# Zeros of a kernel's second sums: one transfer at the end of attention, or twelve pieces along its steps

## The chip, the cores and the metric

The kernel runs on one core of a Trainium2 chip. The metric is the device time of one execution in microseconds (us); less is better. Engines are named as in the profile: PE (TensorE), DVE (VectorE), ACT (ScalarE), POOL (GpSimd) and SP (SyncE, which here only issues DMAs). PEld are PE's weight loads. DMAs are issued from SP, from ACT and, for gathers and scatters, from POOL.

## What is computed

Attention of two kinds is added up (a local one with a band of 7 keys, and one over q, k and v averaged by fours). Its output, 2304 rows of 512, goes through a mixture of experts that takes two of eight experts for each row, and then through a second one that takes one of eight.

```python
def reference(**kwargs):
    attn_out = _attn_ref(**attn_kwargs)               # [4, 8, 576, 64], local + pooled attention
    x = attn_out.transpose(0, 2, 1, 3).reshape(2304, 512)
    x = _moe_ref(x=x, **moe_kwargs)                   # 8 experts, top 2: sum of w * relu(x @ w1[e]) @ w2[e]
    return _moe2_ref(x=x, **moe2_kwargs)              # 8 experts, top 1, with a bias by modality
```

## The kernel before

**Data in DRAM.** `x_rows` (line 878) takes attention's output, a row for each token, and the weights of its two experts. `x2_rows` (line 879), 2944 rows of 516 floats (2304 tokens and 640 spare rows; 2064 bytes each), takes the sums of the first mixture: each expert's results are added to it by scatters that accumulate (line 1220). So it has to hold zeros before the first scatter. In the profile both tensors carry the name `x_rows`. The zeros come from an SBUF tile `zero` that POOL fills at the start (line 936).

**Attention** runs over 16 pairs of heads. Step i of the loop at line 1116 (i from 0 to 17) transposes q and k of pair i+1 (line 193), makes the scores of pair i (lines 211 to 222), the softmax of pair i (`softmax1`, `softmax_d1`, `softmax_d2`) and of i-1 (`softmax2`), and the product with v of pair i-2 (`values`, line 315). Two pairs are a group g; there are eight groups. PE, ACT, DVE and POOL work on a step in turn: PE scores, DVE maxima, ACT exponentials, POOL products (line 269), PE transposes of these (line 283), and so on. In odd steps the loads for the next groups are written: v for the averaged form (`vr`, line 142), and q and k of group g+2 (`qk`: ten DMAs, lines 129 and 132; those of line 132 hold the last 64 positions of all four heads). In even steps v for the local form follows (`vw`, line 156). `group(g+1)` in even steps is the first to use a group's q and k: four transposes of the last 64 positions (line 166), PE's `prs`. A few small inputs are loaded in steps 3 to 7 (lines 923 to 931).

From step 6 on, finished rows of tokens go out: PE transposes them (`px`, line 965), ACT copies them (`xr`, line 986, two buffers; `xrs` for the last five tiles) and issues the write to `x_rows` itself (line 990). The first half's routing (`route1`: DVE, with POOL's help) runs from step 12 on, and SP writes its weights `wb` behind it (line 1031). Behind attention POOL gathers the first expert's rows from `x_rows` (line 709), and the mixture begins: PE transposes of the gathered rows (line 718), ACT `xh` (line 720), and matrix products (lines 735 and 748) to the end of the kernel. Of its weights the first two quarters (`raw`, lines 683 and 684) are loaded by SP as step 14 writes them, and are split into two parts at line 695 (`whi`).

**What sets the order.** The order on each engine is that in which the code is written. SP's queue is one, and in order: a load that waits holds back all that stand behind it. The DMAs of SP and ACT share eight semaphores, taken in turn along the program; a DMA is issued when the one that had its semaphore before has landed, be it of SP or of ACT. SP runs ahead of the other engines by about a step.

**Where the zeros stand.** The whole of `x2_rows` is written with one DMA of SP in step 14, behind the first weights (line 1186). The spare rows of `x_rows` get theirs in step 12 (line 1178).

Of the kernel before, what the change touches and what calls it, by code (L numbers as in the profile page):

```python
# [372 lines left out]
def finish_now(gen):  # L373

    while True:
        try:
            next(gen)
        except StopIteration as e:
            return e.value
# [155 lines left out]
class Items:  # L535
# [94 lines left out]
    def next(self):  # L630

        nc, w, tag, nt = self.nc, self.consts, self.tag, self.nt
        m = w.tile([128, self.most], F32, tag=f"{tag}nm", name="nm")
        j = w.tile([128, self.most], F32, tag=f"{tag}nj", name="nj")
        r = w.tile([128, 1 + nt], F32, tag=f"{tag}nr", name="nr")
        ei = w.tile([128, 1], I32, tag=f"{tag}nei", name="nei")
        nc.vector.tensor_scalar(m, self.ij, self.count, None, op0=ALU.is_equal)
        for a, src in enumerate([self.ei] + [self.col[:, a] for a in range(nt)]):
            nc.vector.tensor_tensor(j, m, src, op=ALU.mult)
            nc.vector.tensor_reduce(r[:, a:a + 1], j, axis=AX.X, op=ALU.add)  # L640
        nc.vector.tensor_copy(ei, r[:, 0:1])
        nc.vector.tensor_scalar(self.count, self.count, 1.0, None, op0=ALU.add)
        return dict(e=ei[0:1], e128=r[:, 0:1], col=[r[:, 1 + a:2 + a] for a in range(nt)])
# [220 lines left out]
def core(ctx, tc, q, k, v, moe_w_gate, moe_w_noise, moe_noise, moe_w1, moe_w2,  # L864
         moe2_modality_id, moe2_w_gate, moe2_modality_bias, moe2_w1, moe2_w2, out):
    nc = tc.nc
# [3 lines left out]
    NT = N // 128  # L870
# [3 lines left out]
    XW, YW = DM + 2 * E, DM + 4  # L874
# [4 lines left out]
    x2_rows = dram.tile([N + 640, YW], F32, tag="x2_rows", name="x2_rows")  # L879
# [29 lines left out]
    with ExitStack() as actx:  # L909
# [25 lines left out]
        zero = consts.tile([128, XW], F32, tag="zero", name="zero")  # L935
# [25 lines left out]
        def xback(t, halves):  # L961

            for o, b, s, n in pieces(t):
                for j in range(4):
                    nc.tensor.matmul(halves[j // 2][o:o + n, j % 2], att.xT[b][:, j, s:s + n], gw[:, j], start=True, stop=True)
            if t < 13:
                return axr.tile([128, 2, 2, 128], F32, tag="xr", name="xr")

            if t == 13:
                many.append(att.sb.tile([128, 5, 2, 2, 128], F32, tag="qk", name="xrs", bufs=2))  # L970

            return many[0][:, NT - 1 - t]
# [3 lines left out]
        def flush():  # L976
            while after:
                after.pop(0)()

        def xback_att(t):  # L980
            px = att.psD.tile([128, 2, 512], F32, tag="D", name="px")
            pv = px[:, :, :2 * XB].rearrange("p a (b c) -> p a b c", b=2)
            xr = xback(t, [pv[:, 0], pv[:, 1]])

            def rest():
                nc.scalar.activation(xr, pv[:, :, :, :128], AF.Copy)
                lgs = axr.tile([128, 2, 2, 2 * E], F32, tag="lgs", name="lgs")
                nc.scalar.activation(lgs, pv[:, :, :, 128:], AF.Copy)
                nc.vector.tensor_reduce(lg[:, t], lgs.rearrange("p a b c -> p c a b"), axis=AX.XY, op=ALU.add)
                nc.scalar.dma_start(x_rows[128 * t:128 * t + 128, :DM], xr.rearrange("p a b c -> p (a b c)"))  # L990
            after.append(rest)
# [63 lines left out]
        def tick(n=1, pe=False):  # L1055

            if pe:
                wait[0] = False
            while n and back and not wait[0]:
                n -= 1  # L1060
                try:
                    what = next(back[0])
                    wait[0] = what in ("PE", "PE soon") and not pe
                    age[0] = 2 if what == "PE soon" else 0
                except StopIteration:
                    back.pop(0)

        def unblock(lag=0):

            if wait[0]:  # L1070
                if age[0] < lag:
                    age[0] += 1
                else:
                    wait[0] = False
                    tick(1)
# [20 lines left out]
        def places_early():  # L1096

            v, f = (t.rearrange("p (e t) -> p e t", e=E)[:, :NX, :NE0] for t in (tab, fs))
            yield from rt.decode(f, v, rt.padh.rearrange("p (e t) -> p e t", e=E)[:, :NX, :NE0])
            nc.vector.tensor_copy(idx0[:, 0], f)  # L1100

            d = route.tile([128, NX, NE0], F32, tag="hold2", name="hold2")
            nc.vector.tensor_scalar(d, f, float(N), -float(N), op0=ALU.is_ge, op1=ALU.mult)
            yield
            nc.vector.tensor_tensor(idx0[:, 1], d, f, op=ALU.add)
            yield
# [9 lines left out]
        for i in range(NP + 2):  # L1116
            g, ph = divmod(i, 2)
            if ph == 1:
                if g + 1 < 2 * B:
                    att.load_vr(g + 1)  # L1120
                if g + 2 < 2 * B:
                    att.load_qk(g + 2)
            if ph == 0 and i and g < 2 * B:
                att.load_vw(g)
            if 3 <= i <= 7:
                next(small, None)
            if i == NP - 1:
                att.pool_v(g, 1)
            if i + 1 < NP:
                if i == 0:  # L1130
                    att.scores(i)
                    att.softmax1(i)
                tr = att.transposes(i + 1)
                next(tr)
            if 1 <= i <= NP:
                att.softmax2(i - 1)
            if i + 1 < NP:
                finish_now(tr)
            if i >= 2:
                att.values(i - 2)  # L1140
                att.scale_d(i - 2)
            flush()
            if i == 12:
                back.append(route1(0, HT, att_bank, nc.vector, nc.gpsimd, hold))
                back.append(places_early())
            unblock(1)
            if i in before:
                xback_att(before[i])
            if 0 < i < NP:
                att.scores(i)  # L1150
            if i >= 2:
                att.combine(i - 2)
            flush()
            tick(2)
            if 1 <= i <= NP:
                pt = att.p_transposes(i - 1)
                next(pt)
            if 0 < i < NP:
                att.softmax1(i)
            if 1 <= i <= NP:  # L1160
                finish_now(pt)
            unblock(1)
            if i < NP:
                att.softmax_d1(i)
                if ph == 0 and g + 1 < 2 * B:
                    att.group(g + 1)
                att.softmax_d2(i)
                for c in ((0,), (1,))[ph] if i > 1 else ((), (0, 1))[ph]:
                    if i < NP - 1:
                        att.pool_v(g, c)  # L1170
            tick(2 if i < NP else 30)
            if i == 9:
                second_bias()
            if i in behind:
                xback_att(behind[i])
            if i == 12:

                nc.sync.dma_start(x_rows[N:].rearrange("(a p) c -> p a c", p=128),
                                  zero[:, None, :].to_broadcast([128, 5, XW]))
            if i == 14:  # L1180
                ffn.begin([dict(e=e, ns=n, w1=moe_w1, w2=moe_w2) for e, n in
                           [(e, EARLY) for e in range(NX)] + [(e, CAP - EARLY) for e in range(NX)]
                           + [(e, CAP) for e in range(NX, LAST)] + [(LAST, 640)]]
                          + [dict(ns=n, w1=moe2_w1, w2=moe2_w2) for n in [512, 256, 256, 384] + [256] * (STATIC - 1)])

                nc.sync.dma_start(x2_rows.rearrange("(a p) c -> p a c", p=128),
                                  zero[:, None, :YW].to_broadcast([128, NT + 5, YW]))
        ffn.start()
        for t in range(13, NT):
            xback_att(t)  # L1190
# [499 lines left out]
```

## Time and profile before

| | |
|---|---|
| median of 3 runs | 907.84 us (905.82 to 912.71) |
| profiled execution: device time | 908.44 us |
| its span, first to last instruction | 906.7 us |
| PE busy | 857.9 us (95%) |
| DVE, ACT, POOL busy | 546.7, 430.3, 318.0 us |
| mean granted TensorE clock | 0.98 |
| DMA | 153.60 MB, mean 169 GB/s |

A busy time is the union of an engine's instructions. In the tables by stretch each row has the stretch, its length, the busy time of PE, PEld, DVE, ACT and POOL with the number of instructions, then the TensorE clock that was granted (1.00 is 2.4 GHz), the mean busy share of the 16 DMA engines and the rate in GB/s (packets are counted where they start, so a share can pass 1). In a timeline a row has start, duration, engine (SPq and ACTq are the issues of DMAs), line, operation, out<-in, and in brackets the idle time of the engine before it and what ended that.

### The profile page before, as it was taken

The numbers are of one execution on the slowest core, as the hardware profiler recorded it, in microseconds if no ns is written. First come the engines' busy times: TensorE is split into PE (matmuls) and PEld (weight loads), VectorE is DVE, ScalarE is ACT, GpSimd is POOL, SyncE is SP. The second block draws the span as 40 slices with busy tenths as digits, with TensorE's granted clock in tenths as the row PEclk, the third lists the DMA queues.
The fourth block names the chain that finished last, engine by engine and source line by source line (L and its number), as shares of the span: only waits on it lengthen the run. The fifth ranks groups of instructions, "written<-read, shape, count | busy, mean of one in ns | idle before, by whom it ended". The sixth has DMA issues, their size and how long they took to land. (4 is left out here: it accounts for less than half of the span.)

```text
span 906.7 us, 18193 instructions
## 1 busy us (share of the span) xinstructions
PE 857.9 (95%) x6775; PEld 752.3 (83%) x6775; DVE 546.7 (60%) x1328; ACT 430.3 (47%) x967; POOL 318.0 (35%) x456
## 2 busy tenths in 40 slices
PE   6898987799999999999999999989989999999995
PEld 5777876688888878889888989977867889999995
DVE  5777799489875545554342433424766877556662
ACT  4576765465554444443342343434324455455562
POOL 7767767355533304314023050140011442222210
PEclk9899999899999999999999999999989999999998
DMA  7868889565776647557147172283514377556650
GB/s 164 181 132 196 194 234 338 180 223 166 250 238 195 152 151 209 126 201 186 60 104 186 47 150 107 59 221 116 164 47 144 136 245 244 187 182 212 212 211 24
DMA packets 158590, 153.60 MB, mean 169 GB/s; under 512 B 74319, under 2 KB 119887, under 8 KB 158496
## 3 DMA queue, kind: packets, MB, share of 16 engines
q1 hardware_dynamic: 142336, 113.33, 41.1%
q0 software_dynamic: 11968, 32.22, 15.3%
q10 hardware_dynamic: 4192, 6.82, 2.1%
q8 instruction: 56, 0.92, 0.4%
q14 instruction: 38, 0.31, 0.1%
HBM read 124.98 MB, written 27.62 MB: 168 GB/s over the span
## 5 line engine op out<-in xcount | busy, mean ns | idle before, releaser
L735 PE MATMUL ph<-xh,whi 128*128 128x256 f32 (+5 forms) x768 | 235.6, 307 | 3.2 <-DVE wlo L696 2.1
L735 PE MATMUL ph<-xl,whi 128*128 128x256 f32 (+5 forms) x768 | 234.8, 306 | 0.5 <-DVE xl L721 0.5
L735 PE MATMUL ph<-xh,wlo 128*128 128x256 f32 (+5 forms) x768 | 234.8, 306 | 0.2 <-DVE wlo L696 0.2
L748 PE MATMUL y<-whi,hh 128*128 128x512 f32 (+1 forms) x472 | 191.7, 406 | 0.0
L696 DVE TENSOR_TENSOR wlo<-raw,whi 128x512 fp32r<-128x512 f32 x135 | 93.3, 691 | 159.7 <-ACT whi L695 153.6
L748 PE MATMUL y<-wlo,hh 128*128 128x512 f32 (+1 forms) x472 | 187.5, 397 | 0.0
L748 PE MATMUL y<-whi,hl 128*128 128x512 f32 (+1 forms) x472 | 187.1, 396 | 0.0
L695 ACT ACTIVATE whi<-raw 128x512 fp32r<-128x512 f32 x160 | 101.0, 631 | 168.2 <-PE y L748 154.3
L735 PEld LDWEIGHTS ph<-xh,whi 128*128 128x128 f32 x768 | 145.2, 189 | 13.6 <-issue 2.6
L735 PEld LDWEIGHTS ph<-xl,whi 128*128 128x128 f32 x768 | 145.3, 189 | 8.5 <-DVE xl L721 1.1
L735 PEld LDWEIGHTS ph<-xh,wlo 128*128 128x128 f32 x768 | 145.5, 189 | 2.1 <-DVE wlo L696 0.6
L737 ACT ACTIVATE hh<-ph 128x256 fp32r<-128x256 f32 (+5 forms) x192 | 82.5, 430 | 136.3 <-PE ph L735 124.8
L738 DVE SCALAR_TENSOR_TENSOR hl<-ph,hh 128x256 fp32r<-128x256 f32 (+5 forms) x192 | 91.5, 477 | 77.7 <-ACT hh L737 75.2
L1220 POOL DMA_INDIRECT x_rows<-y,idx x35 | 57.2, 1634 | 201.6 <-ACT y L1211 104.5
L698 DVE TENSOR_TENSOR wlo<-raw,whi 128x512 fp32r<-128x512 f32 x160 | 119.4, 746 | 12.0 <-ACT whi L697 10.6
L748 PEld LDWEIGHTS y<-whi,hl 128*128 128x128 f32 (+1 forms) x472 | 88.4, 187 | 22.1
L748 PEld LDWEIGHTS y<-whi,hh 128*128 128x128 f32 (+1 forms) x472 | 89.1, 189 | 13.2 <-DVE y L1213 0.2
L748 PEld LDWEIGHTS y<-wlo,hh 128*128 128x128 f32 (+1 forms) x472 | 88.9, 188 | 13.5
L697 ACT ACTIVATE whi<-raw 128x512 fp32r<-128x512 f32 x160 | 98.6, 616 | 0.6 <-DMA raw<-in_moe_w_dram 0.6
L721 DVE TENSOR_TENSOR xl<-pt,xh 128x512 fp32r<-128x512 f32 x59 | 38.6, 687 | 34.1 <-ACT xh L720 33.8
L1220 POOL DMA_INDIRECT out_dram<-y,pi x19 | 20.6, 1084 | 99.8 <-ACT y L1211 43.9
L269 POOL TENSOR_TENSOR Pd<-pe,sm 32x380 f32<-32x380 f32 (+1 forms) x48 | 42.4, 883 | 33.6 <-DVE smd L40 19.0
(311 smaller groups left out, 1074.8 us busy)
## 6 DMA issues: line engine op xcount, KB each, us to landing
raw<-in_moe_w_dram SPq DMA_DIRECT2D x156, 512.0 KB
x_rows<-zero SPq DMA_DIRECT2D x1, 5934.0 KB
vr<-in_v_dram SPq DMA_DIRECT2D x16, 288.0 KB
x2l<-x_rows SPq DMA_DIRECT2D x18, 256.0 KB
qk<-in_q_dram SPq DMA_DIRECT2D x32, 128.0 KB
qk<-in_k_dram SPq DMA_DIRECT2D x32, 128.0 KB
x_rows<-xr ACTq DMA_DIRECT2D x13, 256.0 KB
vw<-in_v_dram SPq DMA_DIRECT2D x24, 128.0 KB
```

Source lines behind the costliest of these rows:

```text
L269: eng.tensor_tensor(Pd[s, :, W * g:W * g + n], pe[s, :, :n], sm[s, :, None].to_broadcast([W, 2 * NB, n]), op=ALU.mult)
L695: nc.scalar.activation(h1, a, AF.Copy)
L696: eng.tensor_tensor(l1, a, h1.bitcast(F32), op=ALU.subtract)
L697: nc.scalar.activation(hi[:, 1], r2[:, half], AF.Copy)
L698: nc.vector.tensor_tensor(lo[:, 1], r2[:, half], hi[:, 1].bitcast(F32), op=ALU.subtract)
L721: nc.vector.tensor_tensor(xl, p, xh.bitcast(F32), op=ALU.subtract)
L735: nc.tensor.matmul(ps, w[a][:, k], x[b][:, k, s], start=(i == 0), stop=(i == 3 * KD - 1))
L737: nc.scalar.activation(hh[:, s], ps, AF.Relu)
L738: nc.vector.scalar_tensor_tensor(hl[:, s], ps, 0.0, hh[:, s].bitcast(F32), op0=ALU.max, op1=ALU.subtract)
L748: nc.tensor.matmul(p[:s.stop - s.start], h[a][:, s], w[b], start=(f == 0 and i == 0), stop=(f == self.FB - 1 and i == 2))
L1220: d = nc.gpsimd.indirect_dma_start(out=dst, out_offset=bass.IndirectOffsetOnAxis(ap=ix, axis=0), in_=y, in_offset=None, **kw)
```

## The change

The one DMA of line 1186 goes. In each of the steps 4 to 15 a DMA of SP takes its place behind the step's other work: it writes zeros to two blocks of 128 rows of `x2_rows`, in step 15 to the one that is left (11 x 2 + 1 = 23 blocks).

```diff
@@ -1173,6 +1173,11 @@
                 second_bias()
             if i in behind:
                 xback_att(behind[i])
+            if 4 <= i <= 15:
+
+                a = range(2 * (i - 4), min(2 * (i - 4) + 2, NT + 5))
+                nc.sync.dma_start(x2_rows[128 * a[0]:128 * (a[-1] + 1)].rearrange("(a p) c -> p a c", p=128),
+                                  zero[:, None, :YW].to_broadcast([128, len(a), YW]))
             if i == 12:
 
                 nc.sync.dma_start(x_rows[N:].rearrange("(a p) c -> p a c", p=128),
@@ -1182,9 +1187,6 @@
-
-                nc.sync.dma_start(x2_rows.rearrange("(a p) c -> p a c", p=128),
-                                  zero[:, None, :YW].to_broadcast([128, NT + 5, YW]))
```

On PE, ACT, DVE and POOL the instructions and their order are the same. On SP the pieces come in between. The first place is SP's queue from the last loads of group 4's q and k (written in step 5) to the first of group 3's `vw` (step 6), before; in brackets stand the semaphores that a row waits for (DMAHW0 to DMAHW7 are the eight):

```order
L132 DMA qk<-in_k_dram 64x4x64 [waits DMAHW0_49]
L129 DMA qk<-in_q_dram 128x4x64 [waits DMAHW1_49]
L129 DMA qk<-in_k_dram 128x4x64 [waits DMAHW2_49]
L129 DMA qk<-in_q_dram 128x4x64 [waits DMAHW3_49]
L129 DMA qk<-in_k_dram 128x4x64 [waits DMAHW4_49]
L928 DMA mid<-in_moe_modality_id_dram 128x18x2 [waits DMAHW5_49]
L156 DMA vw_115<-in_v_dram 125x4x64 [waits DMAHW6_49,PE_49]
```

The same place now; line 1179 is a piece, that of step 5:

```order
L132 DMA qk<-in_k_dram 64x4x64 [waits DMAHW1_49]
L129 DMA qk<-in_q_dram 128x4x64 [waits DMAHW2_49]
L129 DMA qk<-in_k_dram 128x4x64 [waits DMAHW3_49]
L129 DMA qk<-in_q_dram 128x4x64 [waits DMAHW4_49]
L129 DMA qk<-in_k_dram 128x4x64 [waits DMAHW5_49]
L928 DMA mid<-in_moe_modality_id_dram 128x18x2 [waits DMAHW6_49]
L1179 DMA x_rows<-zero 128x2x516 [waits DMAHW7_49]
L156 DMA vw_115<-in_v_dram 125x4x64 [waits DMAHW0_49,PE_49]
```

With the piece of step 4 ahead of them, all have moved on by one semaphore. ACT's first write of token rows, in step 6, took the fifth semaphore before, as ACT's rows there show:

```order
L197 ACTIVATE qT_109<-pq 128x512 [waits DVE_49]
L325 ACTIVATE od<-pva 128x144 [waits PE_49,Activation_49]
L986 ACTIVATE xr<-px 128x512 [waits PE_49]
L988 ACTIVATE lgs<-px 128x64
L990 DMA x_rows<-xr 128x512 [waits DMAHW4_49,Activation_49]
```

Now it has the fourth:

```order
L197 ACTIVATE qT_109<-pq 128x512 [waits DVE_49]
L325 ACTIVATE od<-pva 128x144 [waits PE_49,Activation_49]
L986 ACTIVATE xr<-px 128x512 [waits PE_49]
L988 ACTIVATE lgs<-px 128x64
L990 DMA x_rows<-xr 128x512 [waits DMAHW3_49,Activation_49]
```

So the load that waits for ACT's write was the last of group 4 (the one with DMAHW4 in the first rows), and is now the third from the end (the one with DMAHW3 in the second rows). The second place is SP's queue ahead of group 5's q and k, written in steps 6 and 7, before:

```order
L156 DMA vw_115<-in_v_dram 91x4x64 [waits DMAHW3_49]
L930 DMA g_197<-in_moe_w_gate_dram 128x4x8 [waits DMAHW5_49,DVE_49]
L931 DMA mb<-in_moe_modality_bias_dram 128x16 [waits DMAHW6_49]
L142 DMA vr<-in_v_dram 72x4x256 [waits DMAHW7_49,Pool_49]
L142 DMA vr<-in_v_dram 72x4x256 [waits DMAHW0_49,Pool_49]
L129 DMA qk<-in_q_dram 128x4x64 [waits DMAHW1_49,PE_49]
L129 DMA qk<-in_k_dram 128x4x64 [waits DMAHW2_49]
L129 DMA qk<-in_q_dram 128x4x64 [waits DMAHW3_49]
L129 DMA qk<-in_k_dram 128x4x64 [waits DMAHW4_49]
L132 DMA qk<-in_q_dram 64x4x64 [waits DMAHW6_49]
L132 DMA qk<-in_k_dram 64x4x64 [waits DMAHW7_49]
```

And now, with the piece of step 6:

```order
L156 DMA vw_115<-in_v_dram 91x4x64 [waits DMAHW6_49]
L930 DMA g_197<-in_moe_w_gate_dram 128x4x8 [waits DMAHW7_49,DVE_49]
L931 DMA mb<-in_moe_modality_bias_dram 128x16 [waits DMAHW0_49]
L1179 DMA x_rows<-zero 128x2x516 [waits DMAHW1_49]
L142 DMA vr<-in_v_dram 72x4x256 [waits DMAHW2_49,Pool_49]
L142 DMA vr<-in_v_dram 72x4x256 [waits DMAHW3_49,Pool_49]
L129 DMA qk<-in_q_dram 128x4x64 [waits DMAHW5_49,PE_49]
L129 DMA qk<-in_k_dram 128x4x64 [waits DMAHW6_49]
L129 DMA qk<-in_q_dram 128x4x64 [waits DMAHW7_49]
L129 DMA qk<-in_k_dram 128x4x64 [waits DMAHW0_49]
L132 DMA qk<-in_q_dram 64x4x64 [waits DMAHW1_49]
L132 DMA qk<-in_k_dram 64x4x64 [waits DMAHW2_49]
```

The piece of step 6 stands between the small inputs and `vr`, and the loads of line 132 wait for the semaphores of this piece and of the first `vr` behind it.

## Rows read from the trace of the kernel before

**Rows 1.** The page's first part: each engine's busy time, share, instructions.

```profile
PE 857.9 (95%) x6775; PEld 752.3 (83%) x6775; DVE 546.7 (60%) x1328; ACT 430.3 (47%) x967; POOL 318.0 (35%) x456
```

**Rows 2.** Engines and DMA by stretch: steps 7 to 11, 15, attention's end.

```profile
69.00:76.10 7.10, 7.10 (x155) 6.35 (x154) 5.14 (x14) 5.33 (x19) 4.96 (x7) 1.00 0.82 211
76.10:84.90 8.80, 6.79 (x151) 5.64 (x150) 6.35 (x18) 5.75 (x22) 5.68 (x7) 1.00 0.78 170
84.90:95.00 10.10, 9.01 (x170) 7.78 (x169) 6.66 (x16) 6.03 (x21) 8.77 (x14) 1.00 0.98 185
95.00:103.70 8.70, 8.70 (x166) 7.73 (x165) 7.46 (x23) 6.51 (x23) 5.93 (x8) 1.00 0.81 210
103.70:110.70 7.00, 7.00 (x154) 6.30 (x151) 5.05 (x13) 5.25 (x18) 4.86 (x7) 1.00 0.92 216
...
140.10:149.00 8.90, 5.91 (x115) 4.84 (x116) 8.83 (x28) 3.49 (x10) 8.29 (x12) 0.81 1.06 377
...
131.40:160.30 28.90, 23.41 (x388) 20.07 (x388) 26.53 (x89) 15.46 (x49) 20.43 (x27) 0.94 0.90 308
```

**Rows 3.** Timeline of SP's issues, steps 5 to 14.

```profile
57.56 0.51 SPq L129 DMA_DIRECT2D qk<-in_q_dram  x1
63.27 0.37 SPq L129 DMA_DIRECT2D qk<-in_k_dram  x1
...
78.45 1.57 SPq L132 DMA_DIRECT2D qk<-in_k_dram  x1
...
80.72 0.51 SPq L129 DMA_DIRECT2D qk<-in_k_dram  x1
81.27 0.51 SPq L129 DMA_DIRECT2D qk<-in_q_dram  x1
...
91.36 0.62 SPq L132 DMA_DIRECT2D qk<-in_k_dram  x1
...
108.55 0.60 SPq L132 DMA_DIRECT2D qk<-in_k_dram  x1
...
131.14 0.47 SPq L1186 DMA_DIRECT2D x_rows<-zero  x1
```

**Rows 4.** Timeline of PE: first transposes of groups 5, 6 and 7.

```profile
81.82 0.44 PE L166 MATMUL prs<-gw,qk 64*128 64x64 f32 x4 [1.21 <-ACT pdT L294]
...
98.56 0.46 PE L166 MATMUL prs<-gw,qk 64*128 64x64 f32 x4
...
115.22 0.46 PE L166 MATMUL prs<-gw,qk 64*128 64x64 f32 x4
```

**Rows 5.** SP's wait at 57 to 64 us (sum, times, longest), and ACT's timeline.

```profile
SPq L129 <- DMA x_rows<-xr: 5.2, 1, 5.2
...
61.17 0.37 ACTq L990 DMA_DIRECT2D x_rows<-xr  x1
...
131.23 0.34 ACTq L990 DMA_DIRECT2D x_rows<-xr  x1
...
139.37 0.60 ACT L986 ACTIVATE xr<-px 128x512 f32<-128x512 f32 x1 [0.45 <-DMA x_rows<-xr]
...
141.17 0.60 ACT L986 ACTIVATE xr<-px 128x512 f32<-128x512 f32 x1 [1.09 <-DMA x_rows<-xr]
```

**Rows 6.** Timeline of PE in steps 12 and 13, and the stretch's clock.

```profile
113.38 1.31 PE L283 MATMUL pp<-gw,Pd 128*128 128x128 f32 x10 [0.80 <-POOL Pd L269]
...
122.91 2.39 PE L283 MATMUL pp<-gw,Pd 128*128 128x128 f32 x10 [2.38 <-POOL Pd L269]
...
123.00:127.00 4.00, 4.00 (x25) 3.97 (x26) 3.93 (x13) 1.46 (x4) 3.21 (x4) 0.60 0.68 177
```

**Rows 7.** Timelines behind attention: indices, first gather, first xh.

```profile
158.85 0.17 DVE L1105 TENSOR_TENSOR idx<-hold,fs 128x8 int32<-128x8 f32 x1
...
160.32 1.59 POOL L709 DMA_INDIRECT xg<-x_rows,idx  x1 [6.65 <-DVE wlo L698]
...
168.84 0.60 ACT L720 ACTIVATE xh<-pt 128x512 fp32r<-128x512 f32 x1 [4.70 <-DMA x_rows<-xrs]
```

## The prediction

> **What bounds the kernel now.** I read the page's first lines, then a table of engines and DMA by stretch (step by step), then the timeline of SP beside those of PE, ACT, DVE and POOL around the places that the change touches. TensorE is busy 857.9 of 906.7 us [rows 1]. The change acts ahead of 170 us, so only that part is taken apart. The stretches of [rows 2] begin where PE begins a step's scores (69.00 is step 7, 76.10 step 8, 140.10 step 15). From step 7 to step 11 PE is busy almost throughout, and the DMA engines are busy 0.78 to 0.98 of the time, with no large transfer under way. In step 15, with the whole transfer of zeros in flight, the DMA share is 1.06 at 377 GB/s, but DVE is busy 8.83 of 8.90 us: there the chain is held by VectorE.
>
> How the loads stand to PE is read from two timelines. SP issues them in order [rows 3], and PE first uses a group's q and k in the transposes of line 166 [rows 4]. The last load that these need (line 132, k) is issued at 78.45, 91.36 and 108.55 for groups 5, 6 and 7, and PE begins at 81.82, 98.56 and 115.22: 3.4, 7.2 and 6.7 us later. How much of that is slack depends on the time from issue to landing. On a quiet queue it is 2.1 us: ACT issues the first xr transfer at 61.17, and SP's load at 63.27 had waited 5.2 us for just that [rows 3, 5]. On a full one it is 8.1 us: the transfer of 131.23 lets ACT go on at 139.37 [rows 5]. So group 5 has 0 to 1.3 us of slack (PE's wait of 1.21 us there is put down to ACT, but the data comes at about the same moment), group 6 has 0 to 5.1, group 7 has 0 to 4.6.
>
> **The change, part by part.** One DMA of 128x23x516 floats (6.08 MB) becomes eleven of 528,384 bytes and one of half that. Order and count of instructions on PE, ACT, DVE and POOL stay; SP gets eleven more.
>
> *Price of a piece.* At 377 GB/s [rows 2] a full piece holds the 16 engines for 1.40 us, and SP for about 0.5 us like the whole one (0.47) [rows 3]. What SP waits for grows too: each DMA waits for the landing of the one eight places earlier in program order (the semaphores in the order rows).
>
> On landing time, the rows show 2.1 us for 256 KB on a quiet queue, and yet loads issued every 0.55 us (80.72, 81.27) [rows 3, 5], so these times overlap. The Trainium skill, "DMA: Bandwidth & Descriptors", section "Bandwidth", asks to batch DMAs to at least 1 MiB, and its section "Anatomy of one DMA — SWDGE (gpsimd) path" gives about 2.0 us fixed besides bytes over 436 GB/s. By that an estimate for a piece is 3.2 us, and six pieces in series would hold the queue for 19.3 us, where the stretch's rate gives 8.4. That rule speaks against the change. The sum here goes by the rate; the case of no overlap is a rival below, priced from rows.
>
> *Up to group 5.* SP stands from 58.1 to 63.27 before the last load of group 4, for ACT's transfer [rows 3, 5]. The piece of step 4, which stands ahead of group 4's loads, is absorbed in that pause. In the order rows the same wait now stands two loads earlier, so two loads move behind it: 2 x 0.55 = 1.1 us. Then the pieces of steps 5 and 6 come ahead of group 5's loads: 2 x 1.40 = 2.8. Together 3.9 us. From this go the slack (0 to 1.3) and the idle DMA time of step 7 that might take some up (7.10 x 0.18 = 1.3) [rows 2]: 1.3 to 3.9, and I take 2.8. Queued behind the late loads is everything else of SP; PE, in order, stops at line 166 with the transposes, values and scores of the step behind it, and ACT, DVE and POOL wait for those. So the whole chain moves.
>
> *Up to group 7.* The pieces of steps 7 to 10 add 4 x 1.40 = 5.6, 9.5 us in all. Against it stand DMA idle time from 69.00 to 110.70 (1.3 + 1.9 + 0.2 + 1.7 + 0.6 = 5.7) [rows 2] and group 7's slack (0 to 4.6). The lower bound is what group 5 has already lost, 1.3; the upper is 9.5. I let a quarter of the idle time count (1.4), because SP is itself waiting in it (the load of 78.45 holds SP for 1.57 us, where 0.51 is usual [rows 3]), and a piece in the same queue cannot be issued then. With the middle of the slack (2.3) that leaves **+5.8 us** on attention, of which 2.8 at group 5 and the rest at 6 and 7.
>
> *Behind group 7.* The pieces of steps 11 to 15 lie ahead of no load that is needed soon: the weights are issued ahead of the zeros of 131.14 [rows 3], and nothing reads them before attention's end. Price 0; if that cover were gone, 1.4 us for each piece.
>
> *The clock.* After PE had waited 2.38 us for POOL, its granted clock was 0.60 from 123 to 127 us, so largely the lower of the two levels (1.2 and 2.4 GHz), and the ten transposes took 2.39 us, against 1.31 a step earlier [rows 6]. A wait of 2.8 us at group 5 would do the same: **+1.1 us** (0 if the wait is shorter, 3.3 if all three places do it).
>
> *What the removed transfer gives back.* It is issued at 131.14 and keeps the queue near full to attention's end (share 0.90 from 131.40 to 160.30 [rows 2, 3]). ACT waited for xr transfers 0.45 and 1.09 us [rows 5], but DVE, which ACT feeds there, had no idle time to lose [rows 2]: 0 (at most 1.5). The weights wb of SP's line 1031 go behind the zeros, and POOL's first gather needs them. It begins at 160.32, and its indices were ready at 159.02, so at most 1.3 us is to be had. Behind it ACT's `xh` at 168.84 waits 4.70 us for the last xrs writes [rows 7], which come from attention's last rows and are not the zeros' doing. I take 0.
>
> *Sum.* 5.8 + 1.1 - 0 = +6.9 us. On the profiled execution's 908.44 us (span 906.7) that is 915.3; the median of the three runs, 907.84, lies 0.6 below it, so **914.7 us**. A change of about 1% (9.1 us) is what a measurement of this kernel can tell from none.
>
> **The rivals.**
> - *The loads have room* (chance 0.13). All of the idle DMA time takes up pieces, and attention loses only group 5's 1.3 us; the gather's 1.3 comes back: 907.8. For it: 5.7 us idle. Against it: group 5 has next to no slack.
> - *The queue is full, and the clock falls each time* (0.24). All 9.5 us reach PE, with 3.3 of clock: +12.8, 920.6. For it: the share of 0.98 in step 9 [rows 2], where two pieces more find 0.2 us. It ends slower than 1% once more than 5.8 of the 9.5 us come through with clock losses at all three places.
> - *Pieces do not overlap with what is around them* (0.05). At the quiet 2.1 us per 256 KB [rows 5], a piece is 4.2 us: 6 x 4.2 + 1.1 - 5.7 - 4.6 = +16, or 924. Against it are the loads 0.55 us apart. The Trainium skill's batching rule, named above, would bring this; the trace agrees with its fixed time as latency, not as occupancy.
> - *The end of attention was held by the zeros after all* (0.05). PE's idle time from 131.40 to 160.30 is 28.90 - 23.41 = 5.5 us [rows 2]; if all of it and the gather's 1.3 came back while the loads fit, -6.8: 901. This is the faster side, and its most. Against it: DVE's 8.83 of 8.90.
>
> **How the numbers follow.** My forecast (the chain is some us late, 909 to 917) has 0.53. Slower by over 1% (above 916.9): the second and third rivals, 0.29, and the forecast's upper edge 0.04: 0.33. Faster by over 1% would need 9.1 us where the last rival finds 6.8: 0.02. Within 1%: 0.65. The range that leaves out 2 in 10: from 906, just below the first rival, to 922, just above the second.
>
> **What would show it.** In the profile of the changed kernel: twelve issues of zeros of about 0.5 us; PE's line 166 waiting for q or k loads at group 5 (about 2.8 us) and less at 6 and 7; a granted clock below 1.00 behind the first; step 7 to step 12 with DMA shares near 0.95; scores of step 13 some 6 to 7 us later than before; the same DVE-bound pace from there, with DMA shares well under 1; and the first gather about 7 us after 160.32 [rows 7]. I am wrong if line 166 waits for nothing new (the loads had room), if values or POOL's sums wait first, or if the steps from 131 us on get shorter by more than 1 us (the zeros did hold them).

## The result: slower by 0.9%, by q and k that come late for group 5

The changed kernel takes 917.52 us (median of four runs, 916.35 to 918.43), against 907.36 for the kernel before beside it. The medians lie 10.2 us apart, but the four runs of the kernel before reach from 905.82 to 912.71; by the ratio of the runs, 1.0094 with a 95% interval of 1.0073 to 1.0116, the difference is 8.5 us, and that is the one used here. Run again beside other kernels (below) the ratio was 1.0078 (1.0058 to 1.0099), or 7.1 us. 914.7 us had been forecast, within 906 to 922. The profiled run of the changed kernel is 917.77 us long, its span 916.0.

Line numbers of the changed kernel are the same up to the piece (line 1179), and a few higher behind it. The page's first part answers [rows 1]: PE's busy time is 2.1 us more in a span that is 9.3 us longer.

```profile
PE 860.0 (94%) x6775; PEld 752.7 (82%) x6775; DVE 545.4 (60%) x1328; ACT 430.6 (47%) x967; POOL 316.8 (35%) x456
```

The same work in the same steps, engines and DMA by stretch as in [rows 2], from the scores of steps 7 to 15 on. Columns: stretch and its length, busy time (and count) of PE, PEld, DVE, ACT and POOL, granted clock, DMA share, GB/s.

```profile
70.40:78.60 8.20, 7.27 (x155) 6.28 (x153) 5.94 (x15) 6.17 (x21) 6.00 (x8) 1.00 0.88 236
78.60:92.90 14.30, 9.17 (x150) 7.88 (x148) 6.77 (x18) 5.68 (x21) 6.48 (x8) 0.76 1.01 226
92.90:101.90 9.00, 9.00 (x171) 7.93 (x170) 5.81 (x13) 5.61 (x19) 6.97 (x13) 1.00 0.93 206
101.90:110.60 8.70, 8.70 (x167) 7.73 (x165) 7.46 (x22) 6.51 (x23) 5.92 (x8) 1.00 0.76 210
110.60:117.60 7.00, 7.00 (x154) 6.28 (x153) 5.05 (x13) 5.32 (x19) 4.86 (x7) 1.00 1.00 283
117.60:127.50 9.90, 6.78 (x150) 5.65 (x148) 8.23 (x24) 5.92 (x23) 5.76 (x7) 1.00 0.86 203
...
149.00:157.90 8.90, 5.24 (x115) 3.96 (x115) 8.83 (x27) 3.57 (x11) 8.22 (x12) 0.79 1.03 311
```

Step by step against [rows 2]: step 7 takes 8.20 for 7.10, step 8 14.30 for 8.80, step 9 9.00 for 10.10, and steps 10 and 11 the same 8.70 and 7.00. Step 12 takes 9.90 us for 8.0, and step 15 is as long as before, held by DVE's 8.83 us. Most of the loss is in step 8, with 5.5 us; step 7 adds 1.1 ahead of it, step 9 gives 1.1 back, and step 12 adds 1.9.

What PE waited for from 20 to 180 us (us in all, times, longest), and its timeline at the first transposes of groups 5 and 7, which answers [rows 4]:

```profile
PE prs L166 <- DMA qk<-in_q_dram: 7.4, 2, 5.1
...
PE pva L315 <- DMA vw<-in_v_dram: 0.9, 1, 0.9
```

```profile
87.26 0.85 PE L166 MATMUL prs<-gw,qk 64*128 64x64 f32 x4 [5.13 <-DMA qk<-in_q_dram]
...
92.93 0.34 PE L211 MATMUL pd<-mask,identB 128*128 128x190 bf16 x2
...
124.44 0.50 PE L166 MATMUL prs<-gw,qk 64*128 64x64 f32 x4 [2.31 <-DMA qk<-in_q_dram]
```

The waits for q and k at line 166 are new: 5.13 us at group 5, where 1.21 had been put down to ACT, and 2.31 at group 7; at group 6 there is none. Behind the first of them the work up to step 9's scores takes 92.93 - 87.26 = 5.7 us, against 3.1 before (81.82 to 84.90, [rows 2, 4]). The four transposes take 0.85 us for 0.44, and the granted clock is 0.50, the lower level:

```profile
87.00:91.00 4.00, 3.74 (x22) 3.20 (x24) 2.23 (x8) 2.83 (x12) 0.03 (x1) 0.50 0.97 238
124.00:127.50 3.50, 3.06 (x40) 2.72 (x40) 1.98 (x9) 2.50 (x12) 0.00 (x0) 1.00 0.90 243
```

SP's timeline shows why the loads come late (it answers [rows 3]):

```profile
67.66 1.53 SPq L1179 DMA_DIRECT2D x_rows<-zero  x1
69.28 5.59 SPq L156 DMA_DIRECT2D vw<-in_v_dram  x5
...
75.93 0.42 SPq L1179 DMA_DIRECT2D x_rows<-zero  x1
...
83.07 0.77 SPq L132 DMA_DIRECT2D qk<-in_k_dram  x1
```

The pieces of steps 5 and 6 stand at 67.66 and 75.93. The five value loads of line 156 behind the first take SP 5.59 us, and the last load that group 5 needs goes out at 83.07, 12.7 us behind step 7's scores at 70.40. Before, it was 78.45 - 69.00 = 9.5 us [rows 2, 3]. By the profile SP itself hardly waits for a piece to land, though the loads of line 132 take over the semaphore of one: of its waits from 20 to 180 us only this is put down to the zeros (us in all, times, longest):

```profile
SPq L129 <- DMA x_rows<-zero: 0.3, 1, 0.3
```

At attention's end nothing that counts comes back. ACT's first xh [rows 7] is 8.5 us later than before, and from there to the end of the span it is 738.7 us, against 906.7 - 168.84 = 737.9:

```profile
177.33 0.60 ACT L720 ACTIVATE xh<-pt 128x512 fp32r<-128x512 f32 x1 [4.16 <-DMA x_rows<-xrs]
```

Of those 8.5 us, 1.4 are there when step 7 begins (70.40 for 69.00), and 7.1 come behind it; in the second profile of the changed kernel it is 5.7 us (174.61 - 69.10, for 168.84 - 69.00). The 1.4 repeat in no pattern: step 7 began at 69.10 in the second profile of the same kernel and at 67.40 to 71.30 in the experiments. Profiles are therefore compared from step 7's scores on.

### The profile page after: what moved, and what is told of

It reads as the page before. It is cut to its first block, busy times and chain, and to the rows that moved or that the text cites. A ratio compares the mean times of both kernels' runs of the same rounds, so it can differ in the third digit from the quotient of the medians.

```text
span 916.0 us, 18206 instructions
## 1 busy us (share of the span) xinstructions
PE 860.0 (94%) x6775; PEld 752.7 (82%) x6775; DVE 545.4 (60%) x1328; ACT 430.6 (47%) x967; POOL 316.8 (35%) x456
```

## The experiments

Theory A: the bytes of the pieces of steps 5 and 6 lie ahead of group 5's loads, PE waits for these at line 166, and the clock falls behind the wait. Rivals: what SP issues and waits for costs the time, whatever it carries (C); the split costs wherever it stands (B). All times below are differences from the kernel before beside them (its median, 909.5 to 910.6 us, times the ratio of the runs less one), with 95% intervals. In the three kernels with extra transposes line 166 has become 169, and the lines behind it have moved by 3 likewise.

**Late pieces only.** Five pieces, behind steps 11 to 15:

```
-            if 4 <= i <= 15:
+            if 11 <= i <= 15:
-                a = range(2 * (i - 4), min(2 * (i - 4) + 2, NT + 5))
+                a = range(5 * (i - 11), min(5 * (i - 11) + 5, NT + 5))
```

> The same zeros in five pieces (five blocks of 128 rows each, the last three), one behind each of steps 11 to 15, and none earlier. Theory A (the pieces of steps 4 to 10 hold the DMA queues while the loads of groups 5 and 7 stand behind them): no wait of PE for q or k at line 166, no low clock behind group 5, scores of step 9 within 1.5 us of the kernel before (84.9), and the time within 2 us of before's 907.4. Theory B (the split itself costs, wherever the pieces stand, by SP's extra issues or by the transfer's smaller size): 3 us or more above before, with attention's steps 13 to 15 longer. If the zeros held the last steps after all: 2 us or more below before.

Measured: +1.0 us (-1.1 to +3.0). The stretch of step 8, and PE at line 166:

```profile
77.10:88.20 11.10, 8.62 (x151) 7.18 (x150) 7.66 (x21) 6.31 (x23) 7.21 (x9) 0.85 0.66 157
```

```profile
83.32 0.63 PE L166 MATMUL prs<-gw,qk 64*128 64x64 f32 x4 [1.68 <-DMA qk<-in_q_dram]
```

The time is before's within the interval, so a split into five costs nothing that can be measured behind step 10: B, which asked for 3 us or more, finds no support. Two signs of A failed, though: scores of step 9 came at 88.2, not within 1.5 us of 84.9, and here, too, PE waited for q and k, 1.68 us, and the clock fell. Up to step 10 this kernel's work stands as in the kernel before, so group 5 has next to no slack in either, and two profiles of the same order can differ there by 0.4 us: line 166 begins 13.2 us behind step 7's scores (83.32 - 70.08), for 12.8 before.

**The first three pieces only.** Steps 4 to 6, the rest in one transfer at the old place:

```
-            if 4 <= i <= 15:
+            if 4 <= i <= 6:
...
+                a = range(6, NT + 5)
+                nc.sync.dma_start(x2_rows[128 * a[0]:128 * (a[-1] + 1)].rearrange("(a p) c -> p a c", p=128),
+                                  zero[:, None, :YW].to_broadcast([128, len(a), YW]))
```

> The pieces of steps 4, 5 and 6 as in the changed kernel; the other seventeen blocks in one transfer at the old place. Theory A: PE's wait at line 166 for group 5 stays (about 5 us, as 5.13 in the changed kernel) with the granted clock at 0.50 behind it, none at group 7; 6 to 8 us above before, so 2 to 4 below the changed kernel. Rival (the queue fills up and the late pieces cost as much as the first): half of the loss at most, 3 to 5 us above before.

Measured: +5.5 us (3.7 to 7.2). Engines and DMA by stretch, steps 7, 8 and 12:

```profile
67.70:76.80 9.10, 7.28 (x154) 6.26 (x153) 6.00 (x15) 6.14 (x21) 6.84 (x9) 1.00 0.89 225
76.80:91.50 14.70, 9.37 (x151) 7.96 (x150) 6.42 (x18) 5.74 (x21) 5.79 (x8) 0.77 0.94 208
...
116.10:124.10 8.00, 7.07 (x151) 5.70 (x150) 7.88 (x22) 5.51 (x22) 5.81 (x7) 1.00 0.67 156
```

Steps 7 and 8 look as in the changed kernel (23.8 us together, against 22.5 there and 15.9 before), and step 12 is 8.0 us long as before, with no wait at group 7. So most of the loss is made by three pieces, by way of group 5, as A has it; the time lies just under A's 6 to 8, which its interval reaches.

**Tiny transfers in the pieces' places.**

```
-                nc.sync.dma_start(x2_rows[...], zero[...])
+                nc.sync.dma_start(scratch[128 * (i - 4):128 * (i - 3)], zero[:, :16])
...
```

> In the places of the twelve pieces stand twelve DMAs of 128x16 floats (8 KB) into a scratch tile that nothing reads, extra work; the zeros go in one transfer at the old place. So SP's order and its waits are those of the changed kernel, and the bytes are gone. Theory A (bytes on the queues): wait at line 166 for group 5 of at most 2 us, 1 to 3 us above before. Theory C (SP's order: each DMA more makes the loads behind it wait for a landing eight places earlier, and for ACT's transfer): the wait of about 5 us stays, and 7 us or more above before.

Measured: +2.6 us (1.1 to 4.2). Engines and DMA in steps 7 and 8, and PE at line 166:

```profile
70.50:77.50 7.00, 7.00 (x154) 6.30 (x151) 5.07 (x13) 5.26 (x18) 4.88 (x7) 1.00 0.87 225
77.50:86.30 8.80, 6.88 (x151) 5.69 (x148) 6.34 (x18) 5.77 (x22) 5.75 (x7) 1.00 0.82 174
```

```profile
83.20 0.52 PE L166 MATMUL prs<-gw,qk 64*128 64x64 f32 x4 [1.12 <-ACT pdT L294]
```

Steps 7 and 8 are those of the kernel before to 0.1 us (15.8 for 15.9), though SP issues as many transfers as in the changed kernel. C falls for group 5: there it is the bytes, those of steps 4 to 6 together. The Trainium skill asks to batch DMAs to at least 1 MiB ("DMA: Bandwidth & Descriptors", section "Bandwidth"); if small transfers held up the queue here, these would have delayed steps 7 and 8, and the trace shows none of that. Where the 2.6 us of the whole lie, this run doesn't show. In its profile steps 7 to 12 are as before, and 1.3 us of difference come up between there and the first FFN matmul. Whether the changed kernel, with as many transfers, bears a cost of this kind beside that of the bytes stays open; so does the place of `x2_rows` in DRAM, which the scratch tensor ahead of it may shift.

**The same pieces from ACT's queue.**

```
-                nc.sync.dma_start(x2_rows[...], zero[...])
+                nc.scalar.dma_start(x2_rows[...], zero[...])
```

> The same twelve pieces, issued from ACT's queue instead of SP's. Theory A with the bytes deciding on the shared engines: group 5's loads still land late (wait at line 166 of 3 us or more), 7 us or more above before, and ACT's own 0.5 us an issue may add to it. If it is SP's in-order queue that makes the loads late (a load is not issued before the piece ahead of it is): issues of line 132 for group 5 within 1 us of where they stood to step 7 in the kernel before (78.45, 2.35 behind its scores), wait of at most 2 us, 3 us or less above before.

Measured: +3.0 us (1.4 to 4.6). (The 2.35 us of that text stand behind step 8's scores at 76.10, not step 7's.) ACT's and SP's issues:

```profile
58.81 0.37 ACTq L1179 DMA_DIRECT2D x_rows<-zero  x1
...
66.63 0.37 ACTq L1179 DMA_DIRECT2D x_rows<-zero  x1
```

```profile
57.83 0.60 SPq L132 DMA_DIRECT2D qk<-in_k_dram  x1
63.43 0.38 SPq L129 DMA_DIRECT2D qk<-in_q_dram  x1
...
80.46 0.62 SPq L132 DMA_DIRECT2D qk<-in_k_dram  x1
```

ACT reaches the pieces of steps 5 and 6 some 9 us before SP does (58.81 and 66.63, for 67.66 and 75.93). The first goes into the pause in which SP issues nothing (57.83 to 63.43). Group 5's last load goes out 80.46 - 78.30 = 2.2 us behind step 8's scores, as before (2.35), and PE waits 1.50 us. The time is 3.0 us above before all the same. So the same bytes need not make group 5's loads late: they do when they are issued in SP's order, right ahead of the loads. This run changes both the queue and the moment, and doesn't tell the two apart.

**The changed kernel once more.** No edit.

> The changed kernel as it is, once more, beside the other runs of this set. All theories: 7 to 10 us above before. What it tells is how far the profile repeats: theory A expects PE's wait for q and k at line 166 for group 5 at 4 to 6 us again and the granted clock at 0.50 behind it; the wait for group 7 (2.31 us in the first profile) may vary by 2 us.

Measured: +7.1 us (5.3 to 9.0). Engines and DMA in steps 7 and 8:

```profile
69.10:77.50 8.40, 7.25 (x154) 6.28 (x152) 6.01 (x16) 6.08 (x21) 6.20 (x8) 1.00 0.84 226
77.50:91.10 13.60, 8.56 (x152) 7.38 (x148) 6.34 (x18) 5.77 (x21) 5.80 (x8) 0.75 0.89 221
```

PE's timeline at group 5:

```profile
86.16 0.71 PE L166 MATMUL prs<-gw,qk 64*128 64x64 f32 x4 [5.04 <-DMA qk<-in_q_dram]
```

The wait at group 5 was 5.04 us and at group 7 1.52. Step 9's scores begin 5.0 us behind line 166, for 5.7 in the first profile. Steps 7 and 8 took 22.0 us, against 22.5 in the first profile: the places repeat.

**No piece in step 4.** Steps 5 to 15 carry two blocks each, the last three:

```
-            if 4 <= i <= 15:
+            if 5 <= i <= 15:
...
```

> No piece in step 4; steps 5 to 15 carry two blocks each, the last three. If the piece of step 4 matters (by its 1.4 us, or by the order: it puts SP's wait for ACT's xr transfer, about 62 us, ahead of two loads more): the wait at line 166 for group 5 falls to 3.5 to 4.2 us, and the time to 1 to 2 us below the changed kernel. If it is absorbed in that pause: the same wait (about 5.1) and the same time within 1 us.

Measured: +7.9 us (5.6 to 10.1), with a wait of 4.81 at group 5 in PE's timeline:

```profile
87.30 0.66 PE L166 MATMUL prs<-gw,qk 64*128 64x64 f32 x4 [4.81 <-DMA qk<-in_q_dram]
```

Line 166 begins 87.30 - 70.90 = 16.4 us behind step 7's scores, for 16.9 and 17.1 in the two profiles of the changed kernel. Step 4's piece, with the two loads that it puts behind SP's pause, is worth 0.5 to 0.7 us there, little more than the 0.4 by which two profiles of one order differ, and nothing that shows in the time.

**No pieces in steps 5 and 6.**

```
-            if 4 <= i <= 15:
+            first = {4: 0, 7: 2, 8: 4, 9: 6, 10: 8, 11: 10, 12: 13, 13: 16, 14: 19, 15: 22, 16: 23}
+            if i in first and i < 16:
...
```

> No pieces in steps 5 and 6, the two whose bytes stand ahead of group 5's loads; their blocks go with the pieces of steps 11 to 15 (three blocks each). Pieces of steps 4, 7, 8, 9, 10 as in the changed kernel. Theory A: wait for group 5 at line 166 back to 1 to 2 us, as in the kernel before; then the pieces of steps 7 to 10 meet a PE that is not late: 4 x 1.40 = 5.6 us on the queue less the 4.6 of slack of group 7, so a wait of 1 to 4 us at groups 6 or 7, and 2 to 5 us above before. Rival (only the two pieces ahead of group 5 matter, all others are hidden): no wait at groups 6 and 7, within 1.5 us of before. Rival (every piece costs its share): 5 us or more above before.

Measured: +5.7 us (3.7 to 7.6). Engines and DMA in steps 7, 8 and 12, and PE's timeline at groups 5 and 7:

```profile
67.40:75.10 7.70, 7.23 (x155) 6.24 (x152) 5.75 (x15) 6.00 (x21) 5.57 (x7) 1.00 0.78 198
75.10:86.00 10.90, 8.45 (x151) 7.01 (x150) 6.43 (x19) 5.50 (x21) 6.34 (x9) 0.86 1.04 227
...
111.50:123.00 11.50, 9.56 (x151) 7.87 (x150) 9.75 (x31) 5.95 (x22) 6.22 (x9) 0.74 0.84 214
```

```profile
81.25 0.68 PE L166 MATMUL prs<-gw,qk 64*128 64x64 f32 x4 [2.31 <-DMA qk<-in_q_dram]
...
117.04 1.02 PE L166 MATMUL prs<-gw,qk 64*128 64x64 f32 x4 [1.74 <-DMA qk<-in_q_dram]
```

Group 5's wait falls to 2.31 us (steps 7 and 8: 18.6 us), not quite to A's 1 to 2. Now it is group 7 that waits at the lower clock: step 12 takes 11.5 us. The pieces of steps 7 to 10 are not harmless, as one rival had it. The two parts of the change, +5.5 and +5.7 alone (step 4's piece is in both), don't add up: together they cost 7.1 to 8.5. Once group 5 has made PE late, the loads of groups 6 and 7 have that much more time. The time lies above A's 2 to 5, which its interval reaches; in the profile, whose run was the shortest of its six, 3.2 us more than before come between step 7's scores and the first FFN matmul.

**34 extra transposes ahead of line 166.** In group 5 alone:

```
+        if g == 5:
+            for n in range(34):
+                nc.tensor.transpose(p[:, n % 2].rearrange("p b c -> p (b c)"), self.identF, self.identF)
```

> The changed kernel with extra work: 34 more transposes of the identity on PE ahead of line 166's for group 5, into the bank that those overwrite, so that PE runs on while it waits for q and k. Theory A's clock term (the low clock behind the wait costs 2.6 us: 5.67 us from line 166 to step 9's scores against 3.03 before): granted clock near 1.00 behind the wait, those 5.67 us back to 3.0 to 3.6, the wait itself left as it is, and 2 to 3 us below the changed kernel. If the slow steps behind the wait come from late values or late sums of POOL, and not from the clock: no change.

Measured: +10.5 us (8.5 to 12.6): a miss. The transposes ended too early; PE still waited 1.91 us for q and k, and the clock was 0.71 from 87 to 92 us. Its attention ended as the changed kernel's did. In its profile, that of the longest of its six runs, PE waits 5.6 us for expert weights in one place (line 738), where the changed kernel's longest wait at that line is 2.1 us. Why they come late there, and whether they do in its other runs, stays open. The experts differ from profile to profile in any case: from the first FFN matmul to the end of the span it is 734.9 to 743.9 us in the profiles of all these kernels, this one's the longest.

**52 extra transposes.** The same with `range(52)`.

> As the run with 34 extra transposes, with 52 (at 0.115 us each, from 27 in 3.11 us, they take 6.0 us), so that PE is busy up to the moment when q and k land. Clock theory: wait at line 166 under 1 us, granted clock 1.00 behind it, 3.0 to 3.6 us from there to step 9's scores, 2 to 3 us below the changed kernel in attention (first FFN matmul about 2.5 earlier). If the wait is replaced by as much work and something else (values, sums) holds step 9: no gain. If the loads land later still because of PE's work: a wait again.

Measured: +5.4 us (3.5 to 7.3). SP's last load for group 5, PE's timeline there, then the stretch behind the transposes and step 9:

```profile
81.42 1.66 SPq L132 DMA_DIRECT2D qk<-in_k_dram  x1
```

```profile
81.59 5.89 PE L166 MATMUL prs<-gw 128*128 128x128 f32 x52
87.42 0.46 PE L169 MATMUL prs<-gw,qk 64*128 64x64 f32 x4
...
90.47 0.34 PE L214 MATMUL pd<-mask,identB 128*128 128x190 bf16 x2
```

```profile
87.00:92.00 5.00, 5.00 (x134) 4.23 (x133) 3.54 (x12) 3.02 (x13) 1.39 (x2) 1.00 0.85 220
...
90.50:100.60 10.10, 9.01 (x170) 7.77 (x169) 6.66 (x16) 6.05 (x21) 8.78 (x14) 1.00 1.03 225
```

With PE at work the clock stays at 1.00, and from line 169's transposes to step 9's scores it takes 3.05 us, as before, for 5.7. Those 2.6 us are the clock's. Yet step 9 is 10.10 us long again, as before, where it is 9.00 in the changed kernel: of the 2.6 us, 1.1 come back there. In that step PE waits 1.1 us for POOL's products (line 286), a wait that the changed kernel doesn't have behind its slow step 8. The time is 1.7 us below the repeat's; the intervals overlap, so it doesn't show a gain. Nor does the profile: from step 7's scores to the first FFN matmul it is 107.7 us, for 108.1 and 106.6 in the two of the changed kernel, and the 2 to 3 us less that were expected there did not come. One reason may be that the transposes ran on too long. The last load went out at 81.42, and in the other runs line 166 begins 2.4 to 4.6 us behind that issue; by that the data was there at 83.8 to 86.0, 1.4 to 3.6 us ahead of line 169 (an estimate from those runs).

**The bytes of steps 5 and 6, doubled and halved.** Beside the run with the first three pieces (two blocks of 128 rows in each), four blocks and one block in the pieces of steps 5 and 6, the rest at the old place. For four blocks (for one block the numbers are 0, 2, 3 and 4):

```
-                a = range(2 * (i - 4), 2 * (i - 4) + 2)
+                first = {4: 0, 5: 2, 6: 6, 7: 10}
+                a = range(first[i], first[i + 1])
...
```

> The kernel with pieces in steps 4 to 6 only, but four blocks of rows instead of two in the pieces of steps 5 and 6 (1.06 MB each); the remaining thirteen blocks in one transfer at the old place. Theory A (bytes ahead of group 5's loads, 1.40 us for two blocks): 2.8 us more than with two blocks, so a wait at line 166 for group 5 of 7.5 to 8.5 us (5.33 with two) and 8 to 9 us above before (5.5 with two). Theory C (each DMA costs by its issue and its waits, whatever it carries): wait and time as with two blocks, within 1 us.

> Two blocks in step 4, one in step 5, one in step 6 (264 KB each), the remaining nineteen in one transfer at the old place: half of the bytes ahead of group 5's loads of the kernel with two blocks each, with the same order of the instructions. By a price of 1.40 us for two blocks: 1.4 us less wait at line 166 (about 3.9 for 5.33), 3.5 to 4.5 us above before. If four blocks each cost 1.1 us more than two and that is the price throughout: the wait at 4.7 or more and 5 us above before. If the first blocks cost the most (a slack used up at once, then a step): between the run with tiny transfers and the one with two blocks, with a wait under 3 us and 2 to 4 us above before.

Measured: +6.6 us (4.5 to 8.6) with four blocks, +4.0 (2.2 to 5.7) with one. Steps 7 and 8 with four blocks, PE at line 166, and what else it waited for there (sum, times, longest):

```profile
70.40:81.60 11.20, 8.29 (x155) 7.12 (x153) 6.40 (x17) 6.30 (x21) 8.49 (x10) 0.85 0.86 259
81.60:95.60 14.00, 10.06 (x150) 8.57 (x148) 6.10 (x16) 5.55 (x19) 3.86 (x5) 0.64 0.92 221
```

```profile
90.33 0.66 PE L166 MATMUL prs<-gw,qk 64*128 64x64 f32 x4 [3.94 <-DMA qk<-in_q_dram]
```

```profile
PE pva L315 <- DMA vw<-in_v_dram: 2.9, 1, 2.9
```

Steps 7 and 8 with one block:

```profile
71.30:79.00 7.70, 7.18 (x153) 6.20 (x151) 5.75 (x15) 6.02 (x21) 5.57 (x7) 1.00 0.82 218
79.00:92.70 13.70, 9.46 (x150) 7.88 (x148) 6.94 (x19) 5.75 (x21) 6.96 (x10) 0.77 0.90 199
```

PE at line 166 with one block, and in the run with the first three pieces (two blocks in each):

```profile
87.00 0.80 PE L166 MATMUL prs<-gw,qk 64*128 64x64 f32 x4 [4.16 <-DMA qk<-in_q_dram]
```

```profile
85.70 0.86 PE L166 MATMUL prs<-gw,qk 64*128 64x64 f32 x4 [5.33 <-DMA qk<-in_q_dram]
```

Four blocks split the wait: 2.9 us fall on the values (line 315, whose loads stand behind step 5's piece), and only 3.94 are left at line 166, not 7.5 to 8.5; the time, too, is below A's 8 to 9, which its interval reaches. A wait alone is thus no measure. What serves is the time from step 7's scores to line 166's transposes:

- 12.7 us with tiny transfers in all places, step 4's too;
- 13.9 with step 4's piece and none in steps 5 and 6 (81.25 - 67.40), where step 7's piece goes out just ahead and may add a little;
- 15.7 with one block in each of steps 5 and 6 (87.00 - 71.30);
- 16.9 to 18.0 with two (87.26 - 70.40, 85.70 - 67.70);
- 19.9 with four (90.33 - 70.40).

From one block to two (0.53 MB more) it is 1.2 to 2.3 us, and from two to four (1.06 MB) 1.9 to 3.0, so 0.9 to 1.5 for each 0.53 MB. For the first 0.53 MB it is 1.8 us from the row with step 4's piece, and 3.0 from the tiny transfers, but that difference holds step 4's 0.53 MB as well. From 13.9 to 19.9 the mean is 1.5 us for each 0.53 MB, near the 1.40 of the prediction. Without step 4's piece, two blocks cost 3.2 to 3.7 us (16.4 for 12.7 to 13.2), or 1.6 to 1.9 for each 0.53 MB. One block had a wait of 4.16 us and +4.0 us in all: the price of 1.40 had about 3.9 and 3.5 to 4.5, while "the first blocks cost the most" asked for a wait under 3 us. So the cost goes by the bytes, at about that price; that the first block costs more than the next is not shown. The times, +4.0, +5.5 and +6.6, rise with the bytes too, but one step lies within the intervals of the next.

**The kernel before with 12 extra transposes** in the same place:

```
+            for n in range(12):
```

> The kernel before with 12 extra transposes (1.4 us) on PE ahead of line 166's for group 5, overwritten by those. If the kernel before itself loses to the low clock there in part of its executions (late5, whose order is the same up to step 10, waited 1.68 us, with the clock at 0.72 behind it and 4.9 us to step 9's scores where before has 3.1): 0.5 to 2 us below before. If not: within 1 us of it, or above by the extra work.

Measured: +0.1 us (-1.8 to +2.0). In its profile, that of the shortest of its twelve runs, the transposes take 1.5 us and fill the gap, nothing waits at line 169, and the clock stays at 1.00, but no gain can be measured:

```profile
81.37 0.46 PE L169 MATMUL prs<-gw,qk 64*128 64x64 f32 x4
```

No kernel here is faster than the one before.

## Why the prediction was right, and where its terms were not

- **Direction and place: right.** PE waits for q and k at line 166, worst at group 5, with a low clock behind it. From step 7's scores to the first xh the first profile is 7.1 us above before's and the repeat's 5.7, and the repeat's time lies 7.1 above before; 6.9 were forecast. The first measurement, 8.5 us by its ratio, holds 6.9 in its interval (6.6 to 10.5).
- **Group 5: too small.** 2.8 us were taken, 3.9 less 1.1 for slack and idle DMA time. Line 166 stands 4.0 to 4.2 us further behind step 7's scores (16.9 and 17.1 for 12.8): the 3.9 was nearly right, and nothing should have been taken off. The step that failed is that a DMA share of 0.82 in step 7 would take up part of the pieces. The share is an average; the pieces stand in SP's order between loads that already come just in time, as the run with late pieces shows by its own wait of 1.68 us. Of the parts of the 3.9, the two loads shifted by step 4's piece are worth 0.5 to 0.7 where it is left out (1.0 by the run without the pieces of steps 5 and 6), where 1.1 was forecast, and the pieces of steps 5 and 6 3.2 to 3.7 rather than 2.8.
- **Price of a piece, 1.40 us: near, a little low.** The runs give 0.9 to 2.3 us for each two blocks and 1.5 in the mean from none to four; the two pieces without step 4's cost 1.6 to 1.9 each.
- **Values: not foreseen as a cost.** I named a wait of the values ahead of line 166 as a sign of error. It came (0.9 us in the first profile, 1.8 with the first three pieces), since step 5's piece stands ahead of line 156's loads. It is the same delay met one step earlier: step 7 grows by 1.1, and the wait at line 166 is shorter for it.
- **The clock, +1.1: right in sum.** 2.6 us are lost behind the wait in the first profile (5.7 for 3.1) and 1.9 in the repeat (5.0), and 1.1 and 1.2 come back in step 9: 1.5 and 0.7. The bound of 3.3 for three low clocks was not reached, because behind group 7's wait of 2.31 us the clock stayed at 1.00.
- **Groups 6 and 7, 3.0 us more behind group 5: too much.** Group 6 waits for nothing, steps 10 and 11 are as long as before, and group 7's wait is 2.31 and 1.52 us, of which step 12 shows 1.9 in the first profile and 0.8 in the repeat (9.90 and 8.80 for 8.0). The error at group 5 and this one largely cancel, so the total came out nearer than its parts, which is luck. The run without pieces in steps 5 and 6 fits this: there group 5 is less late, and step 12 takes 11.5 us for 9.90 and 8.80, so PE's lateness is room for the later loads.
- **The removed transfer, 0, and the pieces of steps 11 to 15, 0: in line with the runs.** Step 15 is 8.90 us long as before with DVE at 8.83, and late pieces alone cost +1.0 (-1.1 to +3.0).
- **The rivals.** "The loads have room" (907.8) falls with the waits. "The queue is full, and the clock falls each time" (920.6) overstates group 7. "Pieces do not overlap" (924) falls with the price: about 1.5 us for each piece, for its 4.2; a fixed time for each transfer in the queue falls with steps 7 and 8 of the tiny transfers. (The fixed time that the prediction takes from the Trainium skill, "DMA: Bandwidth & Descriptors", section "Anatomy of one DMA — SWDGE (gpsimd) path", is given there for DMAs that POOL issues; the pieces are SP's.) "The zeros held attention's end" (901) falls with step 15.

## What to carry to other kernels

Five pieces behind the last critical loads cost nothing that could be measured here, and the same bytes cost where they were issued ahead of loads that come just in time. So look for each consumer's slack from issue to use before placing a piece, price it by its bytes, and don't count the idle share of the DMA engines as room. Delays in a chain of prefetches need not add up: here the first late group handed its lateness to the later ones as slack. After a stall, also look one step further: part of a low clock's cost may come back where another engine was to be waited for anyway.

## What the runs showed of the hardware that was not expected

- The length of a wait does not alone tell the clock behind it. After 2.31 us at group 5 (the run without pieces in steps 5 and 6) step 8 had a granted clock of 0.86; after 2.31 us at group 7 of the changed kernel it stayed at 1.00 in step 12 and from 124.0 to 127.5. Waits of 1.12 us (tiny transfers) left it at 1.00, 1.68 (late pieces) brought step 8 to 0.85, and with PE kept at work by 52 transposes it was 1.00.
- Twelve transfers of 8 KB in SP's queue, most of them at 0.4 to 0.6 us of SP, left steps 7 and 8 as they were to 0.1 us, and yet the kernel was 2.6 us (1.1 to 4.2) slower, by a cause that its profile doesn't name.
- The same bytes issued from ACT's queue, some 9 us earlier in steps 5 and 6 and one piece of them in a pause of SP, cost 3.0 us in place of 7.1 to 8.5.
